# A gated convolution block with an MLP on one core: a short convolution in 8 steps of 16 channels, a skip term added before the transposes, two more tiles through the transposing DMA, paired 64-row matmuls, and a new order

## The chip, the core and the metric

One core of a Trainium2 chip runs the whole program. The metric is the time of one execution on the device in microseconds (us), the median of several runs. The engines have these names: PE (TensorE, matmuls; PEld are its weight loads), DVE (VectorE), ACT (ScalarE), POOL (GpSimd) and SP, which here issues DMAs. Each engine works through its own list of instructions in order; semaphores make one wait for another. PE writes to PSUM, which has 8 banks here (128 partitions x 512 float32 columns); only DVE and ACT empty them.

## The reference

S = 2048 positions, D = 640 channels, F = 1728, all inputs bfloat16:

```python
x = A_q
# A: short convolution, gate, long convolution, skip term, gate
k_shift[t] = sum(k[t - j] * shift_k[:, j] for j in range(4))      # per channel
kv = k_shift * v
y  = long_conv(kv, ssm_k) + kv * ssm_D                            # causal, 2048 taps, per channel (an FFT in the reference)
h  = x + layernorm(x) * y
# B: MLP
a  = layernorm(h) @ w1 + b1;  act = a * tanh(softplus(a))         # Mish
out = h + act @ w2
```

## The kernel before

The long convolution is done as matmuls with constant tables, in two steps forward (128 x 16), a product per frequency, and two steps back. `s1kpe`, `s1vpe` are the first forward step of the filter and of `kv` (lines L543 and L544: pairs of matmuls that each use 64 columns of the array and run together), `s2kpe` (L652) and `s2vpe` (L685) the second with the 4 MB table `g`, `p1_`/`p2_` (L706, L710) the products, `i1pe` (L743, L744) and `i2pa/b/c` (L803) the way back. `k1pe` (L625) transposes the filter, `ktpe` (L571) transposes k. Channels go in five blocks of 128 that form chunks 0 (blocks 0, 1), 1 (2, 3) and 2 (4). `sw` are DMAs inside SBUF that swap neighbouring partitions of the filter's spectrum for the complex product.

The short convolution `kspe` (L595, L596) multiplies transposed k with banded matrices `wsh`, which POOL builds (L501) from `coef`, a spread-out copy of shift_k (L493). Four steps of 32 channels by 4 times: a first matmul of 128 columns and a second of 96 columns that brings in the time steps before. `kv` (L600, DVE) takes the result out of PSUM and multiplies it by v. The skip term is one addition to the transposed filter's first row, `dadd` (L620), behind the `k1` transposes.

After the way back, for each of 16 tiles of 128 positions: `y` moves it out of PSUM (L419 on ACT, L421 on DVE), `wb` (L813) multiplies by the normed x (`lnx`, L790 on ACT or L792 on POOL), `h` (L817) adds x, `bn` (L822 to L824) and `pow` (L827, POOL) give the statistics, `hc` (L832) the normed tile. Tiles 0 to 3 are transposed by PE (`trpe`, L850) and copied (`trev`), tiles 4 to 15 by a transposing DMA (`trd`, L839). The MLP runs in five units of 256, 256, 512, 512, 512 positions: `m1pe` (L898) is the first matmul for 13 blocks of 128 hidden values, `m1pex` (L878) that for the last 64 of 1728 (two halves of positions together), `hb`/`hbx` (L903, L881) Mish on ACT, `m2pe` (L915, L916) the second matmul with 14 accumulating steps for each half of a tile, `res` (L921) the residual and `d_out` the way out. The 14th step (L916) holds 64 hidden values and 64 rows of zeros, which POOL writes (`w2z`, `w2hz`).

What runs where and in which order is written out by hand: the string `ORDER` names some 700 operations with an engine letter (t PE, a ACT, v DVE, p POOL, d a DMA issued by SP, s one issued by ACT). `_schedule` gives each a start from a table of costs and sorts by it; the lists of the engines come out of that. SP's DMAs are one list too: a DMA whose wait is not over holds up all behind it. `fz` and `wm` are matmuls on zeros whose results nothing uses. A POOL product that overlaps DVE's products is put behind them by a copy into `turn` (L936), since `_schedule` gives products of the two engines one port.

Of the kernel before, what the change touches and what calls it, by code (L numbers as in the profile page):

```python
# [17 lines left out]
D = 640  # L18
# [8 lines left out]
d_id:s d_sk:s wz:v d_dr:s cz:v d_go:d d_n2:d wm:t fz0:t d_n0:d k1pe2x:t warm:a k1ev2x:a d_n3:d k1pe2y:t d_n1:d cfpe:t d_n4:d k1pe0y:t k1ev0y:a  # L27
k1pe0x:t k1ev2y:v dadd2:v s1kpe2_0x:t k1ev0x:v kz:p coef:v s1kpe2_2x:t s1kpe2_1x:t s1kpe2_1y:t s1kev2_1x:v s1kev2_0x:v s1kev2_1y:v s1kpe2_3y:t
s1kev2_3y:a k1pe3x:t k1ev3x:a s1kev2_2x:a k1pe1x:t k1ev1x:v k1pe1y:t w2hz:p dadd0:p wsh0:p dadd1:p k1pe3y:t dadd3:p k1pe4y:t k1ev1y:v k1pe4x:t
k1ev3y:v k1ev4x:v dadd4:p s1kpe1_2y:t k1ev4y:a s1kpe1_3x:t s1kpe1_0x:t s1kev1_0x:v s1kpe1_0y:t s1kpe1_1x:t s1kev1_1x:v s1kpe0_1x:t s1kpe1_3y:t  # L30
s1kpe4_0y:t s1kev1_2y:a s1kpe2_2y:t s1kev1_3x:a d_k3:d d_k2:d d_x0:d s1kev0_1x:a s1kev1_0y:v s1kev1_3y:a s1kev2_2y:a s1kpe3_0x:t s1kpe0_2y:t
s1kev0_2y:a s1kpe0_1y:t s1kev3_0x:a s1kpe2_3x:t s1kev2_3x:a ktpe3y:t s1kpe0_2x:t s1kpe4_2x:t s1kev4_2x:a s1kev4_0y:v ln1_2:v s1kev0_1y:v ln1_1:v
s1kpe4_1x:t s1kpe0_0x:t s1kev4_1x:a s1kpe4_2y:t s1kpe1_2x:t s1kev0_0x:v s1kpe0_0y:t d_k1:d d_g4:d s1kev1_2x:a d_k0:d d_g5:d s1kpe3_2x:t ktpe0y:t
s1kev0_2x:a ktpe1y:t d_v1:d ktev0y:v ktpe4y:t ktev3y:v s1kpe4_0x:t ktev1y:v ktev4y:v s1kev4_2y:a s1kev0_0y:a s1kev3_2x:a s1kpe3_1y:t s1kev4_0x:a
s1kev3_1y:a s1kpe3_3x:t s1kpe3_0y:t s1kpe4_1y:t s1kev3_3x:a s1kpe0_3y:t s1kpe4_3y:t s1kpe2_0y:t s1kpe4_3x:t s1kev0_3y:v s1kev2_0y:v s1kev4_1y:a
ln1_3:v s1kev3_0y:a s1kev4_3x:a wsh1:p s1kpe3_2y:t ln1p1:p s1kpe3_1x:t s1kpe1_1y:t ktsh1:p wsh3:p s1kpe0_3x:t s1kpe3_3y:t s1kev3_1x:a ktpe2y:t
s1kev0_3x:a s1kev4_3y:a s1kev3_2y:v s1kev1_1y:v ktpe4x:t ktpe3x:t ktev3x:v ktpe1x:t s1kev3_3y:a ktev1x:v ln1_0:v ktpe0x:t s2kpe_14y:t d_g6:d d_g0:d
ktev2y:a ktpe2x:t d_g7:d d_g1:d ktev4x:a s2kpe_13x:t s2kev_13x:a s2kpe_15y:t s2kpe_12y:t s2kev_12y:a ktev0x:a s2kev_15y:a kspe4_1x:t ktev2x:v kv4_1x:v
kspe1_1y:t s2kpe_11y:t kv1_1y:v kspe1_1x:t s2kev_11y:a kspe4_1y:t kv1_1x:v s2kpe_1y:t s2kev_1y:a kv4_1y:v ktsh0:p wsh2:p s2kpe_12x:t kspe0_1y:t
kv0_1y:v s2kpe_13y:t s2kpe_16y:t kspe3_1x:t s2kpe_16x:t kv3_1x:v s2kev_12x:a s2kev_14y:a s2kev_16x:v d_v0:d s2kev_16y:a d_g3:d s2kev_13y:a kspe0_1x:t  # L40
kv0_1x:v s2kpe_19y:t d_g2:d ktsh4:p s2kpe_0y:t s2kpe_0x:t s2kev_0x:a s2kpe_1x:t s2kev_1x:a s2kev_0y:a d_small:p ktsh3:p s2kev_19y:a ktsh2:p kspe3_1y:t
kv3_1y:v kspe2_1x:t s2kpe_18x:t s2kev_18x:a s2kpe_20y:t kv2_1x:v s2kpe_17x:t s2kpe_18y:t s2kpe_17y:t s2kpe_4y:t s2kev_17x:a s2kev_20y:v s2kpe_3x:t
# [132 lines left out]
def _schedule(ops):  # L175
# [7 lines left out]
    for word in ORDER:  # L183
# [32 lines left out]
        for rt in o.allocs:  # L216
            rt.ring.take(rt.slot, rt)
# [751 lines left out]
```

## Time and profile before

| | us |
|---|---|
| median of 3 runs (224.56 to 224.84) | 224.58 |
| the profiled execution | 224.86 |
| its span, first to last instruction | 223.1 |
| PE busy | 214.7 (96%) |
| DVE busy | 146.2 (66%) |
| ACT busy | 134.4 (60%) |
| POOL busy | 65.7 (29%) |

The granted TensorE clock is 1.000 throughout. "Busy" of PE counts the overlapping lengths of pipelined matmuls (a 128-column one is 219 ns long, but the next starts 56 ns later), so a PE that is always busy can still issue less than it could. Starts in the timeline show the rate. The span starts with the first instruction; some 1.8 us of the execution lie outside it.

### The profile page before, as it was taken

What the parts mean: (1) busy time and instruction counts of PE and PEld (TensorE: products, weight loads), DVE (VectorE), ACT (ScalarE), POOL (GpSimd) and SP (SyncE); (2) the same over time, 40 slices, a digit from 0 to 9 for tenths busy, and PEclk for the clock granted to TensorE, in tenths of its full rate; (3) what the DMA queues carried; (4) which work ended last, traced back from release to release, by engine and by line L of the source; (5) the groups of instructions that cost most, each with busy time, mean ns of one, the idle gap of its engine ahead of it and who ended that gap; (6) DMA issues with size and microseconds to landing.
All of it is one profiled execution on the core that took longest, in us unless ns stands there. A gap on an engine that the chain in (4) does not pass through costs nothing.

```text
span 223.1 us, 6218 instructions
## 1 busy us (share of the span) xinstructions
PE 214.7 (96%) x2598; PEld 162.1 (73%) x2598; DVE 146.2 (66%) x317; ACT 134.4 (60%) x268; POOL 65.7 (29%) x106
## 2 busy tenths in 40 slices
PE   7998899999999999999999999999999999999994
PEld 2988899999877999988887644576645445675773
DVE  0699989999999998999788898974400000004023
ACT  2689989999999999888870446800053454330000
POOL 1271950005596007235767714320000000000000
PEclk9999999999999999999999999999999999999999
DMA  6999991075999999100001401043350000000024
GB/s 214 388 408 424 408 413 69 3 203 193 277 290 283 319 351 347 62 3 0 3 0 32 88 0 31 0 91 60 88 179 0 1 0 3 0 0 0 32 82 153
DMA packets 27342, 30.68 MB, mean 138 GB/s; under 512 B 9393, under 2 KB 23730, under 8 KB 26930
## 3 DMA queue, kind: packets, MB, share of 16 engines
q1 hardware_dynamic: 26880, 30.10, 41.1%
q8 instruction: 20, 0.33, 0.6%
q10 hardware_dynamic: 338, 0.18, 0.3%
q14 instruction: 8, 0.07, 0.1%
q0 software_dynamic: 96, 0.00, 0.0%
HBM read 20.45 MB, written 2.62 MB: 103 GB/s over the span
## 4 chain that ended last, share of the span: by engine, by line
PE 64%; DVE 13%; DMA 7%; ACT 7%; POOL 5%; issue 2%; SPq 0%; DVEq 0%; ACTq 0%; POOLq 0%
PE ps L915 21%; PE ps L898 19%; ACT uv L419 6%; DMA x<-in_A_q_dram 5%; PE ps L743 4%; PE ps L744 4%; PE ps L652 3%; PE ps L543 2%; PE ps L571 2%; DMA rn<-in_A_ssm_k_dram 2%; DVE st L776 2%; DVE st L822 2%; PE ps L595 2%; POOL r L782 2%; PE ps L916 2%
## 5 line engine op out<-in xcount | busy, mean ns | idle before, releaser
L915 PE MATMUL ps<-rn,uv 128*128 128x320 bf16 (+2 forms) x416 | 61.1, 299 | 0.2 <-DVE x L921 0.2
L903 ACT ACTIVATE uv<-ps,b1s 128x512 bf16<-128x512 f32 (+1 forms) x65 | 35.4, 610 | 39.1 <-PE ps L898 38.5
L898 PE MATMUL ps<-G 128*128 128x512 bf16 (+1 forms) x325 | 58.6, 337 | 0.0
L915 PEld LDWEIGHTS <-uv 128*128 128x128 bf16 x416 | 40.2, 98 | 17.5 <-issue 0.4
L419 ACT CAST uk<-ps 128x512 bf16<-128x512 f32 (+1 forms) x96 | 48.7, 702 | 2.6 <-PE ps L544 1.6
L898 PEld LDWEIGHTS <-G 128*128 128x128 bf16 x325 | 31.2, 98 | 23.9 <-issue 1.1
L921 DVE TENSOR_TENSOR xb<-ps,xb 128x320 bf16<-128x320 f32 (+2 forms) x12 | 5.7, 487 | 36.3 <-PE ps L916 35.8
L419 ACT CAST uv<-ps 128x512 bf16<-128x512 f32 (+2 forms) x57 | 28.7, 845 | 0.0
L921 DVE TENSOR_TENSOR xa<-ps,xa 128x320 bf16<-128x320 f32 x12 | 5.9, 488 | 21.6 <-PE ps L916 21.6
L827 POOL TENSOR_TENSOR r<-ve,mhalf 128x1 f32<-128x1 f32 x16 | 10.0, 630 | 32.7 <-DVE ve L824 32.7
L743 PE MATMUL ps<-a,uv 128*128 128x128 bf16 x160 | 18.8, 219 | 0.2
L421 DVE CAST uk<-ps 128x512 bf16<-128x512 f32 (+1 forms) x27 | 17.2, 669 | 1.4 <-PE ps L744 0.9
L743 PEld LDWEIGHTS <-uv 128*128 128x128 bf16 x160 | 17.9, 113 | 0.0
L421 DVE CAST uv<-ps 128x512 bf16<-128x512 f32 (+1 forms) x25 | 15.3, 677 | 0.0
L685 PE MATMUL ps<-uv,G 128*128 128x64 bf16 (+1 forms) x256 | 12.8, 197 | 0.8
L685 PEld LDWEIGHTS <-G 128*128 128x128 bf16 x256 | 11.1, 96 | 3.1 <-issue 2.1
L600 DVE TENSOR_TENSOR ra<-ps,rb 128x512 bf16<-128x512 f32 x20 | 12.5, 684 | 0.3 <-PE ps L596 0.3
L419 ACT CAST rb<-ps 128x512 bf16<-128x512 f32 (+1 forms) x28 | 10.6, 495 | 2.7 <-PE ps L803 2.7
L652 PE MATMUL ps<-uk,G 128*128 128x160 bf16 x128 | 12.1, 230 | 0.0
L782 POOL TENSOR_TENSOR r<-ve,mhalf 128x1 f32<-128x1 f32 x16 | 10.8, 672 | 1.3
L706 DVE TENSOR_TENSOR uv<-uv,uk 128x2048 bf16<-128x2048 bf16 (+1 forms) x11 | 10.9, 1022 | 0.0
L544 PE MATMUL ps<-cst,ra 128*64 128x128 bf16 x160 | 10.6, 220 | 0.1
(116 smaller groups left out, 376.7 us busy)
## 6 DMA issues: line engine op xcount, KB each, us to landing
G<-tab_g SPq DMA_DIRECT2D x8, 512.0 KB, 12.9
rn<-in_A_ssm_k_dram SPq DMA_DIRECT2D x5, 512.0 KB, 6.2
ra<-in_A_k_dram SPq DMA_DIRECT2D x4, 640.0 KB, 9.9
rb<-in_A_v_dram SPq DMA_DIRECT2D x2, 1280.0 KB, 13.1
G<-in_B_w_dram SPq DMA_DIRECT2D x5, 432.0 KB, 6.4
rn<-in_B_w_dram SPq DMA_DIRECT2D x1, 2080.0 KB, 9.8
rn<-uk SPq DMA_DIRECT2D x4, 512.0 KB, 5.1
rb<-uk SPq DMA_DIRECT2D x8, 256.0 KB, 7.9
```

The costliest lines, as they stand in the source:

```text
L419: nc.scalar.copy(o, i)
L421: nc.vector.tensor_copy(o, i)
L600: nc.vector.tensor_tensor(kv_w[:, m, :, 8 * h:8 * h + 8, l0:l0 + n], ps.rearrange("p (l t d) -> p d t l", l=n, t=8), raw_v[:, 8 * h:8 * h ...
L652: nc.tensor.matmul(ps[:, o:o + 160], g_v[:, f, :], KA[:, :, f, :], start=True, stop=True)
L685: nc.tensor.matmul(ps[:, fl * n:fl * n + n], g_v[:, f0 + h * kf + fl, :], VX[x][:, :, f0 + h * kf + fl, :], start=True, stop=True)
L706: eng.tensor_tensor(v, v, K[c.i][:, :, f0:f1, :], ALU.mult)
L743: nc.tensor.matmul(pz[:, k, :], V[c.i][:, dg // 4, :, dg % 4], a12[:, 0, :], start=True, stop=False)
L782: nc.gpsimd.tensor_tensor(r1[:, t2:t2 + 1], ve1[:, t2:t2 + 1], mhalf[:, 0:1], ALU.pow)
L898: nc.tensor.matmul(ph[:, 0:w], w1[:, dc, fc * P:fc * P + P], lnhT_of(u)[:, dc, 0:w], start=(dc == 0), stop=(dc == NDC - 1))
L903: nc.scalar.activation(hb_of(u)[:, fc, 0:w], rt.tile[:, 0:w], ACT.Mish, bias=b1s[:, fc:fc + 1], scale=1.0)
L915: nc.tensor.matmul(po[:, 0:d1 - d0], hb_of(u)[:, fc, tl * P:(tl + 1) * P], w2[:, fc, d0:d1], start=(fc == 0), stop=False)
L921: nc.vector.tensor_tensor(x, rt.tile[:, 0:d1 - d0], x, ALU.add)
```

## The change

- **Short convolution.** 8 steps of 16 channels. k is transposed so that a bank holds channels of one parity; the second matmul has 48 columns instead of 96. `wsh` is 10 pieces of 704 columns (5 blocks, 2 parities) instead of 4 of 1120; five of them lie in the `uv` tiles, five in `xb`. `coef` comes out of nine small matmuls (`cfpe`) as one copy of 440 columns; before, it was a memset and four copies. `ktsh`, the shift by one row on POOL, has 1016 elements instead of 508.
- **Skip term.** Four small matmuls (`dcpe`) and a copy (`dcev`, 5 columns) spread ssm_D over the partitions, and `dq` (DVE, 128 x 1, five times) adds it to the filter before the transposes; the `dadd` go.
- **Tiles 2 and 3** are transposed by DMA (`trd2`, `trd3`).
- **The last 64 hidden values.** `m2q` multiplies them first, for two tiles at a time: each matmul uses 64 rows of the array, one tile the lower half, the other the upper, with 4 banks taken per pair. `m2pe` keeps 13 steps. The zero rows and their memsets go. `m1pex` does each unit by itself in the same number of columns.
- **Products of chunk 0** in 8 pieces of 1024 elements instead of 4 of 2048, and their `sw` DMAs in 4 pieces instead of 2.
- **Loads.** Half of the first filter block comes from ACT's queue. `fz` is two matmuls instead of one, `wm` 8 instead of 9.
- **Order.** All of `ORDER` is new. On SP the filter blocks come first, then x0 after one quarter of k, v earlier, the table g in the order of use; `w2` is behind `trd3`, where before it stood ahead of x1. Of the products POOL has 9 of 1024 elements (before 2 of 2048), and DVE 23 of 1024 and 4 of 2048 (before 16 and 10).

```diff
-ORDER = """d_id:s d_sk:s wz:v d_dr:s cz:v d_go:d d_n2:d wm:t fz0:t d_n0:d k1pe2x:t ...
+ORDER = """wz:v kz:p d_id:s d_sk:s d_go:d d_n0:d d_n1:d wm:t dcpe:t dcev:v dq0:v fz1:t k1pe0y:t k1pe0x:t cfpe:t ...
...
+    for a in range(4):   # emit_dc
+        nc.tensor.matmul(ps_f32(dc_rt)[:, 0:NDC], cst[0:32, 4 * P + 3 - a:5 * P + 3 - a], d_row[:, a:20:4], start=(a == 0), stop=(a == 3))
...
-            m = mk.unsqueeze(1).to_broadcast([P, 35, 32])
+            out = wsh[m][k].rearrange("p l (t d) -> p (l t) d", d=16)
+            a = mk.unsqueeze(1).to_broadcast([P, 44, 16])
...
-                        nc.tensor.matmul(o, t[:, l, a, :], wsh[r // 5][:, r % 5, 0:128], start=True, stop=False)
-                        nc.tensor.matmul(o[:, 0:96], t[:, l, a - 1 if a else 4, :], wsh[r // 5][:, r % 5, 128:224], start=False, stop=True)
+                    nc.tensor.matmul(o, t[:, q, h, :], w[:, 0:128], start=True, stop=False)
+                    nc.tensor.matmul(o[:, 0:48], t[:, q, 0 if h else 2, :], w[:, 128:176], start=False, stop=True)
...
-            k = kd[0:1, 0]
-            (nc.vector if e == "dve" else nc.gpsimd).tensor_tensor(k, k, rd, ALU.add)
+            nc.vector.tensor_tensor(n[:, 0:1], n[:, 0:1], d_col[:, b:b + 1], ALU.add)
...
-        npf = (32, 32, 32)[len(c.dcs) - 1]
+        npf = (16, 32, 32)[c.i]
...
-        if U_OF[t2] >= 2:
+        if U_OF[t2] >= 1:
...
+            def pq(e, ab=ab, parts=parts):
+                for i in range(2):
+                    for t2 in ab:
+                        _, c, h = last64[t2]
+                        d0, d1, rt = parts[t2][i]
+                        rhs = w2h[64:P, d0:d1] if h else w2[0:64, 13, d0:d1]
+                        nc.tensor.matmul(ps_f32(rt)[:, 0:d1 - d0], hbx[64 * h:64 * h + 64, c:c + P], rhs, start=True, stop=False)
...
-                    for fc in range(NFC - 1):
-                        nc.tensor.matmul(po[:, 0:d1 - d0], hb_of(u)[:, fc, tl * P:(tl + 1) * P], w2[:, fc, d0:d1], start=(fc == 0), stop=False)
-                    nc.tensor.matmul(po[:, 0:d1 - d0], lhs, w2h[:, d0:d1] if h else w2[:, 13, d0:d1], start=False, stop=True)
+                    for fc in range(NFC - 1):
+                        nc.tensor.matmul(po[:, 0:d1 - d0], hb_of(u)[:, fc, tl * P:(tl + 1) * P], w2[:, fc, d0:d1], start=False, stop=(fc == NFC - 2))
```

More of the change, by code (lines that the diff above doesn't have):

```diff
@@ L26 @@
 ORDER = """
[L27 to L30, printed above, removed]
@@ L71 @@
-i2pa2:t i1ev2_3x:v y0a:a ln1_15:v i2pc0:t y0b:v i2pc1:t y1a:a ln1p2:p lnx0:p lnx2:p i2pa9:t y1b:a wb0:v wb1:v i2pa12:t h0:v h1:v bn0:v bn1:v i2pb2:t
-i2pa6:t i2pa8:t i2pb6:t i2pa3:t i2pa11:t pow0:p y6a:a i2pa15:t i2pb11:t i2pb15:t i2pb3:t hc0:v i2pc2:t pow1:p y2a:a d_x1:d y11a:a y15a:v i2pa14:t
-i2pb8:t y2b:a y3a:a hc1:v i2pb14:t i2pb12:t i2pa10:t i2pa7:t i2pc3:t y14a:a y12a:a y8a:a y3b:a i2pb9:t i2pb10:t i2pa5:t i2pc6:t y6b:a i2pb7:t i2pb5:t
-i2pc7:t trpe0:t i2pa13:t i2pa4:t y9a:a trev0:v trpe1:t y7a:a y10a:a y7b:v trev1:v wb3:v wb2:v h3:v i2pc11:t i2pb4:t i2pc12:t i2pc9:t i2pb13:t
@@ L75 @@
-m1pe0_9:t y5a:a y4a:a y11b:a hb0_9:a h2:v bn2:v bn3:v ln1p15:p m1pe0_4:t y9b:a m1pe0_5:t m1pe0_3:t m1pe0_6:t i2pc4:t y4b:a hb0_6:a m1pe0_11:t
-m1pe0_2:t pow2:p hc2:v m1pe0_0:t pow3:p ln1_6:v hc3:v y12b:a m1pe0_10:t ln1p6:p lnx6:p ln1_12:v ln1_4:v ln1_5:v hb0_5:a y13a:a hb0_4:a hb0_10:a w2z:p
-trpe2:t hb0_0:a hb0_2:a trev2:a m1pe0_7:t ln1p5:p m1pe0_8:t trpe3:t trev3:a ln1p4:p m1pe0_12:t m1pe0_1:t hb0_7:a hb0_8:a hb0_1:a hb0_3:a m1pex0:t
-m1pe1_8:t wb6:v h6:v m1pe1_11:t ln1_8:v hb0_12:a i2pc8:t lnx4:p m1pe1_10:t y8b:a hb0_11:a hb1_11:a m1pe1_7:t hb1_7:a m1pe1_2:t m1pe1_5:t m1pe1_6:t
@@ L95 @@
-d_out12:d d_out8:d d_out4:d d_out13:d
+wz:v kz:p d_id:s d_sk:s d_go:d d_n0:d d_n1:d wm:t dcpe:t dcev:v dq0:v fz1:t k1pe0y:t k1pe0x:t cfpe:t k1pe1y:t warm:a k1ev0x:v k1ev0y:a s1kpe0_3y:t
+s1kev0_3y:a s1kpe0_2y:t s1kpe0_0x:t coef:v wsh4_0:p wsh1_1:p wsh2_0:p dq1:v wsh0_0:p wsh3_0:p wsh1_0:p s1kpe0_0y:t d_n3:d d_n2:d s1kpe0_1y:t
+s1kpe0_3x:t s1kpe0_1x:t k1ev1y:a wsh2_1:p wsh4_1:p wsh3_1:p wsh0_1:p s1kev0_0y:v dq3:v s1kev0_0x:v dq2:v d_n4:d d_k3:d d_x0:d d_k2:d k1pe1x:t k1pe2y:t
+k1pe2x:t s1kev0_1y:a k1ev1x:a k1ev2y:v dq4:v k1pe3y:t k1pe3x:t k1ev3y:v k1ev2x:v k1ev3x:a fz0:t s1kev0_3x:a s1kpe1_2y:t s1kpe1_1y:t s1kev0_1x:v d_k0:d
@@ new lines @@
+i1ev1_2y:v i1ev2_3x:v i1pe2_2y:t i1ev2_2y:v i2pa0:t i2pa1:t i2pb0:t i2pa2:t i2pb1:t y1a:a i2pc0:t i2pc1:t y1b:a i2pa7:t y0a:v y0b:v wb0:v wb1:v
+i2pb2:t i2pa8:t y2a:a c_b1:a h0:v h1:v bn0:v bn1:v d_w10:d d_w13:d i2pb7:t d_w12:d d_x1:d d_w11:d y7a:a pow0:p i2pa3:t i2pb8:t i2pa9:t i2pc2:t i2pb3:t
+y3a:a i2pa4:t i2pb9:t i2pc6:t i2pa12:t y2b:a i2pb4:t y8a:a pow1:p i2pa10:t hc0:v i2pa6:t i2pa11:t i2pa13:t i2pb6:t y9a:a y4a:a y6a:a i2pb11:t i2pa5:t
+i2pb10:t i2pb13:t i2pc3:t y6b:a y3b:a wb2:v y13a:a hc1:v fz2:t trpe0:t i2pa15:t i2pa14:t wb3:v h2:v trpe1:t h3:v bn2:v trev0:a pow2:p bn3:v pow3:p
@@ new lines @@
+i2pb14:t i2pb15:t i2pb5:t i2pb12:t trev1:a i2pc4:t y4b:a m1pe0_7:t y14a:a m1pe0_6:t hb0_7:a hc2:v trd2:d hc3:v trd3:d ln1_6:v y15a:a d_w2:d hb0_6:a
+y10a:a ln1p11:p ln1p6:p m1pe0_0:t m1pe0_2:t m1pe0_11:t i2pc5:t y11a:a y5a:a hb0_2:a hb0_0:a m1pe0_4:t m1pe0_3:t i2pc14:t m1pe0_1:t hb0_4:a y5b:v
+hb0_3:a ln1_7:v hb0_11:a lnx6:p ln1p7:p ln1_4:v ln1_5:v lnx11:p ln1p5:p y14b:v m1pe0_5:t m1pe0_12:t hb0_12:a i2pc13:t y13b:v m1pe0_10:t y12a:a hb0_5:a
+ln1_12:v ln1_8:v i2pc11:t m1pe0_9:t m1pe0_8:t i2pc8:t hb0_10:a m1pe1_11:t y11b:a hb1_11:a hb0_1:a lnx5:p m1pe1_4:t y8b:v m1pe1_3:t hb0_8:a hb1_3:a
@@ L187, in _schedule @@
         dur = dict(o.opts)[eng]
-        est = max([free.get(eng, 0.0)] + [d.finish + d.lat + _TAIL[d.eng] + _HOP for d in o.deps])
+        est = max([free.get(eng, 0.0)] + [d.finish + (0.0 if d.eng == eng and eng.startswith("dma") else d.lat + _TAIL[d.eng] + _HOP) for d in o.deps])
         base = est
@@ L191, in _schedule @@
             t, rt.slot = rt.ring.free()
+            rt.ring.take(rt.slot, rt)
             est = max(est, t)
@@ L204, in _schedule @@
                     t = fetched
-                fetched = t + (_SLOW if free.get("dma", 0.0) > t + 0.3 else _FETCH)
+                fetched = t + next(d for end, d in _FETCH if t < end)
                 mark += _BLOCK
@@ L327 @@
     turn = cpool.tile([P, 1], BF16, name="turn")
-    sk_r = cpool.tile([32, 80], BF16, name="sk_r")
-    coef = cpool.tile([P, 20, 7], BF16, name="coef")
+    sk_r = cpool.tile([16, 160], BF16, name="sk_r")
+    d_col = cpool.tile([P, NDC], BF16, name="d_col")
+    d_row = cpool.tile([32, 20], BF16, name="d_row")
+    coef = cpool.tile([P, 440], BF16, name="coef")
     st1 = cpool.tile([P, NT, 2, 6], F32, name="st1")
@@ L530 @@
     d_go = OP("d_go", ("dma", 0.75))
-    d_n = [DMA(f"d_n{b}", P * S * 2, emit_kn(b), deps=[d_go], lat=3.1) for b in range(NDC)]
+    d_n = [DMA("d_n0", P * S * 2, emit_kn(0), deps=[d_go], rate=405e3, lat=3.0)]
+    d_n += [DMA(f"d_n{b}", P * S * 2, emit_kn(b), deps=d_n[:1], rate=405e3, lat=3.45) for b in range(1, NDC)]
+    for o in d_k + d_v:
+        o.deps.append(d_n[0])
     s1_pes = [[] for _ in CHUNKS]
@@ L584, in shf @@
         def shf(e, t=kt_s[b]):
-            nc.gpsimd.tensor_copy(t[:, :, 4, 1:128], t[:, :, 3, 0:127])
-        kts.append((o_ev, OP(f"ktsh{b}", ("pool", 0.61), [o for o in o_ev if not o.name.endswith("x")], emit=shf, prio=9)))
+            nc.gpsimd.tensor_copy(t[:, :, 2, 1:128], t[:, :, 1, 0:127])
+        kts.append((o_ev, OP(f"ktsh{b}", ("pool", 1.1), [o for o in o_ev if not o.name.endswith("x")], emit=shf, prio=9)))
     for m in range(NDC):
@@ L605 @@
             ks_pe_all += o_pe
             kv_ops[m] += o_kv
-    d_g = [DMA(f"d_g{i}", 0.525e6, emit_g(i), prio=0.6, lat=4.9) for i in range(8)]
+    d_g = [DMA(f"d_g{i}", 0.525e6, emit_g(i), deps=d_n[:1], prio=0.6, lat=4.9) for i in range(8)]
     d_small = OP("d_small", ("pool", 3.0), kts[0][0], emit=emit_small2, lat=6.0)
@@ L712 @@
             extra = 0.06 * (len(SW[c.i]) - 1)
[L713 removed]
+            p2 = OP(f"p2_{c.i}_{i}", [("dve", _dve2(npf * n) + extra), ("pool", _pool2(npf * n) + extra)], need + [o for k, o in enumerate(sw_ops[c.i]) if k * P // len(sw_ops[c.i]) < f1 and (k + 1) * P // len(sw_ops[c.i]) > f0], emit=(lambda e, fn=fn: fn(e, which=1)), prio=15 + c.i)
             p2.probe = SW[c.i][-1][1][:, 0, f1 - 1, 0:1]
@@ L754, in emit_x @@
         return lambda: nc.sync.dma_start((x0, xa, xb)[h][:, 0:(4, 6, 6)[h] * D].rearrange("p (a d) -> p a d", d=D), xview[:, (0, 4, 10)[h]:(4, 10, 16)[h], :])
-    d_x = [DMA(f"d_x{h}", (0.66e6, 0.98e6, 0.98e6)[h], emit_x(h), deps=((), i1_pes[1], ks_pe_all)[h], prio=3.5 if h else 0.55, lat=2.5 if h else 3.4) for h in range(3)]
+    d_x = [DMA(f"d_x{h}", (0.66e6, 0.98e6, 0.98e6)[h], emit_x(h), deps=(d_n[:1], i1_pes[1], ks_pe_all)[h], prio=3.5 if h else 0.55, lat=2.5 if h else 3.4) for h in range(3)]
     def emit_w2():
```

284 lines of the change are left out of this document (146 added, 138 removed).

## Prediction

> **What bounds the kernel now.** First the page's 40 slices, then busy time by stretch.
>
> ```profile
> PE   7998899999999999999999999999999999999994
> DVE  0699989999999998999788898974400000004023
> ACT  2689989999999999888870446800053454330000
> DMA  6999991075999999100001401043350000000024
> ```
>
> PE looks full everywhere, so the other rows divide the span: DVE and ACT are full too until about slice 15, and fall off after.
>
> ```profile
> core 0: us, PE busy (x) PEld busy (x) DVE busy (x) ACT busy (x) POOL busy (x), PEclk, DMA share, GB/s
> 5.70:28.00 22.30, 20.39 (x472) 19.32 (x473) 19.72 (x41) 19.05 (x33) 12.58 (x14) 1.00 1.02 407
> 28.00:50.00 22.00, 22.00 (x452) 21.43 (x451) 21.23 (x37) 21.19 (x46) 3.17 (x7) 1.00 0.49 173
> 50.00:72.70 22.70, 21.11 (x464) 18.36 (x462) 22.54 (x32) 22.70 (x50) 14.94 (x9) 1.00 0.90 259
> 72.70:124.00 51.30, 51.16 (x612) 45.37 (x612) 46.53 (x115) 39.98 (x92) 23.50 (x46) 1.00 0.37 121
> 124.00:220.00 96.00, 95.87 (x595) 56.30 (x594) 35.36 (x94) 30.00 (x49) 10.48 (x21) 1.00 0.16 41
> ```
>
> Up to 72.7 us the copies out of PSUM bind: DVE and ACT stand still for 7.4 us of engine time between 5.7 and 50 us and for 0.2 us between 50 and 72.7. From 72.7 us PE binds; DVE and ACT have room. The chain of waits gives PE's rate there, start to start, and the cost of going over to matmuls on half the array:
>
> ```profile
> 51.02 0.96 PE ps L685 x32
> ...
> 128.10 3.36 PE ps L898 x15
> 131.46 0.67 PE ps L878 x10
> ...
> 143.13 1.77 PE ps L915 x13
> 145.03 1.77 PE ps L915 x13
> ...
> 168.88 14.03 PE ps L898 x65
> ```
>
> A 512-column matmul costs 14.03/65 = 0.216 us, a 320-column one 1.77/13 = 0.136, a 64-column one 0.03. The 15 before L878 take 3.36 where 15 x 0.216 = 3.24: 0.12 is the way in. The 10 halves of 256 columns run in pairs, 5 x 0.109 = 0.55, and take 0.67: 0.12 is the way out. So a visit costs 0.24.
>
> **The change, part by part.** Two sums, since only what the bound engine saves counts.
>
> *PE's stretch, after 72.7 us.* (1) The 14th step goes: 30 x 0.136 + 0.216 + 0.056 = 4.35. The pairs cost half that, 2.18, if they overlap as the column halves of L878 do, and eight visits cost 8 x 0.24 = 1.92: net -0.25. No row shows row halves; the bounds are 2.18 less (switches free) and 2.18 more (no overlap); I take L878's row as the nearest. (2) `trpe2`, `trpe3`: 10 transposes at 0.056 us, start to start: -0.56. What hides the DMA instead (2.6 us from issue to landing, SP 1.2 us each) is `m1pe0`. With hc1's end as zero, DVE needs 0.8 for two `h` and 0.4 for a `wb`, 2.6 for two `bn` and 0.4 for `hc2`: 4.2. `hc3` ends at 4.8, its DMA is issued by 5.5 and lands at 8.1. PE reaches unit 1 after `trpe1` and `trev1` (1.5), 13 x 0.545 and five `i2pc` (0.11 each): 9.1. Cover 1.0 us, so nothing is charged. (3) `fz2` doubles ahead of `trpe0`: +0.2 of its 0.43, as PE waits there for `hc0` in part. (4) `w2` is now issued behind `trd3`, at 6.7. It is 2.2 MB; x1 moved at 404 GB/s (7,680-byte packets), w2's 1,280-byte packets at about 370, so 6 us and some 2 us to start and end: 14.7 to 15. PE comes to `m2q0`, which needs its last rows, after eight `m1pe1` and `m1pex0`: 9.1 + 8 x 0.545 + 0.79 + 0.11 = 14.4. All of `m1pe1` and `m2pe` queues behind it: +0.5. Sum: -0.25 - 0.56 + 0.2 + 0.5 = **-0.1**.
>
> *The copies' stretch, before.* (5) DVE's products: from 10 x 1.14 + 16 x 0.60 = 21.0 to 4 x 1.14 + 23 x 0.60 = 18.4: -2.6; POOL takes nine halves of the 4.1 us that L710 shows, 18.4 instead of 8.1, in a stretch where it is busy 15 of 45 us. (6) `coef`: four copies of 0.24 and a 0.175 memset become one copy of about 0.55: -0.6; the DVE `dadd`, -0.2. (7) `dq` and `dcev`: six small DVE instructions at 0.15 (a 128x1 row): +0.9. Together -2.5 for two engines that share the copies: **-1.2**. (8) The 48 columns save PE 80 x (0.042 - 0.029) = 1.0, where PE is not the bound: 0 (bound -1.0). `cfpe`, `dcpe`, `wm` lie ahead of the first landing: 0. `wsh` is 10 x 1.3 = 13 us of POOL instead of 8.3, `ktsh` 1.2 instead of 0.61; the first user, `kspe0_1y`, comes behind all filter blocks, near 28 us: 0. (9) `dq0` stands ahead of `k1pe0x`: a copy, an addition, two hops: +0.2; `k1pe0y` covers the rest. (10) `dq1` to `dq4` have two operands in SBUF and run while POOL builds `wsh`. The timelines of POOL and DVE show what that does:
>
> ```profile
> 114.02 0.87 POOL L792 TENSOR_SCALAR ra<-xa,r,nmr 128x640 bf16<-128x640 bf16 x1
> 114.29 0.94 DVE L813 TENSOR_TENSOR rb<-rb,ra 128x640 bf16<-128x640 bf16 x1
> 116.03 0.48 DVE L813 TENSOR_TENSOR rb<-rb,ra 128x640 bf16<-128x640 bf16 x1
> ```
>
> The addition that met POOL's instruction took 0.94 instead of 0.48. Each `dq` can wait out a piece of `wsh`: 0 to 1.3, mean 0.65, and the copies behind it on DVE wait too, with PE behind those banks. 4 x 0.65 = 2.6 on DVE, some of it in idle time that is there anyway: +0.6. The Trainium skill (SBUF — State Buffer, section "Who interferes with whom") says that a DVE instruction with two SBUF inputs and a GpSimd one that reads SBUF exclude each other for the whole instruction; by that rule all four wait and the term is nearer its upper end. (11) The order. Of the 7.4 idle us some 2.1 are the wait for the first bank (ACT 6.48, DVE 6.98); 5.3 are left, with the wait for x0 (0.6 on DVE) and a stall of PE's instruction supply (0.8 at L571) among them. x0 now comes one k quarter earlier, v before most of g, and the chunk 0 path starts ahead of the filter's last blocks. I let half be filled, 5.3 / 2 / 2 = -1.3; ends 0 and -2.65, or +2 if the new lists stall elsewhere. (12) Quarters of `sw0` have 256-byte pieces: the transposes' 256-byte packets took 18 ns, the swaps' 512-byte ones 28, so 2 MB cost 9.2 us of DMA instead of 7.2, beside a DMA that the 28 to 50 stretch shows half idle: 0. Sum: -1.2 + 0.2 + 0.6 - 1.3 = **-1.7**.
>
> The profiled execution, 224.86, becomes 224.86 - 1.8 = 223.06; it stood 0.28 over the median: 222.8.
>
> **Rivals.**
>
> *Slower, w2 late.* In before w2's last pieces landed 8.3 and 9.7 us after issue, on a busy DMA. If they do so here, from 7.9, they land at 16.2 to 17.6 and PE stands at `m2q0` until then: 3.2 us instead of 0.5, so 225.5. It decides from a wait of 2.3 on, which eats the whole gain. Against it: DMA is idle then (0.03 of its time from 90 to 100 us). Chance 0.14.
>
> *Slower, the shared port.* By the skill's rule above, as this kernel's mechanism: four `dq` wait 1.3 each (5.2), and DVE's products beside POOL's three late ones another 2. DVE, in order, is then 7 late against 2.5 saved, and ACT cannot take its copies: +4.5 instead of -0.6 for terms 5 to 7 and 10, halved where ACT has spare banks: 225.6. For it: the 0.94 above. Against: at 63 to 70 us POOL's small instructions, not DVE's, were stretched. 0.14.
>
> *The pairs do not pair.* Row halves in one column pass run one after the other: +2.18, 225.0, within 0.2% of now. 0.10.
>
> *More gain.* Idle time all filled, no lock, free switches: -1.35 - 0.6 - 1.9 - 0.5 = 218.4. The new lists may also take PE's stalls of 50 to 72.7 us (22.7 less 21.11 busy, more by start times). 0.18.
>
> **Numbers.** Forecast 222.8, chance 0.44. About 0.2%, 0.45 us, is what a measurement of this kernel can tell from no change. Faster: 0.44 + 0.18 = 0.62; same 0.10; slower 0.28. The range takes in both slow rivals with the bound of term 11 and most of the gain: 218.4 to 226.4; the forecast's own case spans 220.5 to 224.1.
>
> **What would show it.** Right: 13 steps in 1.77 us with 16 pairs at 0.136 and 0.24 per visit; DVE and ACT idle under 6 us from 5.7 to 50; PE full from about 71 us; under 1 us of wait for a DMA at `m2q0`. Wrong: `dq` rows of 0.6 us and more, PE waiting for `w2` or for a transposed tile, 0.27 us between pairs, or DVE waiting in 50 to 73 us.

## The result, and the profile after

| | before | after |
|---|---|---|
| median, us | 224.57 (224.19 to 224.84, 4 runs) | 232.76 (231.92 to 234.07, 4 runs) |
| profiled execution, its span | 224.86, 223.1 | 234.07, 232.3 |
| granted TensorE clock | 1.000 | 0.978 |

The ratio is 1.0371, 95% interval 1.0320 to 1.0422: slower by 8.2 us. The forecast was 222.8.

The 40 slices of the page, changed kernel (tenths; one slice is 5.8 us):

```profile
PE   7689999999988999999959999999999999999994
...
DVE  0269999999999999998976678935341000032131
ACT  2156998999999999899862232830113287300000
...
PEclk9679999999999999999988999999999999999999
DMA  6999179434499990512921610243024000000034
```

Two places stand out (slices counted from 0), and PEclk, which was 9 throughout before, marks both: slices 1 and 2, where DVE and ACT are half idle, and slice 20, where PE falls to 5 and the clock to 8 for two slices. The windows put sizes to them (columns as in the prediction; the last three are granted clock, DMA share, GB/s):

```profile
5.70:28.00 22.30, 19.03 (x323) 17.05 (x324) 14.90 (x29) 12.91 (x20) 13.31 (x10) 0.85 0.84 329
28.00:50.00 22.00, 21.60 (x502) 20.18 (x497) 21.40 (x38) 21.27 (x45) 10.08 (x16) 1.00 0.69 233
...
72.70:124.00 51.30, 48.29 (x629) 43.19 (x629) 48.21 (x113) 44.83 (x99) 22.25 (x39) 0.97 0.55 182
```

From 5.7 to 28 us DVE has 14.9 us of work done (before 19.72), ACT 12.9 (before 19.05), at a clock of 0.85. After that the stages run at their old pace: the first `kspe` starts at 35.27 instead of 29.42, 5.9 later; the first `m1pe` at 103.76 instead of 98.05, 5.7 later. From there to the end it takes 128.5 instead of 125.05, and what is lost lies around the first `m2q`.

PE's waits name both (engine, line and what it waited for: us in total, times, longest):

```profile
PE ps L930 <- ACT uv L914: 2.8, 1, 2.8
PE ps L634 <- DMA rn<-in_A_ssm_k_dram: 2.4, 1, 2.4
...
PE ps L634 <- DVE rn L628: 1.0, 1, 1.0
```

L634 is `k1pe`, waiting for the first filter block and then for `dq` (L628); L930 is `m2q`. The DMA issues show why the first block is late: of its two halves the one in ACT's queue, third there, is issued at 1.63 and takes 6.2 us, to 7.9; SP's half, issued at 0.72, lands at 4.6.

```profile
rn<-in_A_ssm_k_dram SPq DMA_DIRECT2D x1, 256.0 KB, 3.9
rn<-in_A_ssm_k_dram ACTq DMA_DIRECT2D x1, 256.0 KB, 6.2
```

The first `s1kpe` pairs start 0.107 us apart (12.2 to 14.9 us) and 0.056 in the groups after 19 us; before they were at 0.056 in the first group already. The chain shows the same thing behind the second wait, and further on a visit to `m2q` in its normal state:

```profile
120.26 1.74 PE ps L909 x10
122.00 2.89 PE ps L942 x13
...
125.55 1.77 PE ps L942 x13
127.32 1.09 PE ps L909 x10
...
130.18 0.38 PE ps L930 x4
130.55 1.87 PE ps L942 x13
```

Ten `m1pe` matmuls take 1.74 instead of 1.09, a half tile of `m2pe` 2.89 instead of 1.77: 1.8 us lost after the wait was over.

### The profile page after: what moved, and what is told of

The parts are those of the page before. It is cut to its first block, busy times and chain, and to the rows that moved or that the text cites. A ratio compares the mean times of both kernels' runs of the same rounds, so it can differ in the third digit from the quotient of the medians.

```text
span 232.3 us, 6302 instructions
## 1 busy us (share of the span) xinstructions
PE 219.9 (95%) x2623; PEld 162.3 (70%) x2623; DVE 146.7 (63%) x324; ACT 133.2 (57%) x261; POOL 78.9 (34%) x114
## 4 chain that ended last, share of the span: by engine, by line
PE 55%; POOL 5%; DVE 4%; issue 1%; ACT 1%; DVEq 0%; POOLq 0%
PE ps L942 25%; PE ps L909 20%; PE ps L754 4%; PE ps L755 4%; POOL r L791 2%; PE ps L930 1%; DVE st L831 1%; POOL ra L801 1%; POOL nmr L792 1%; PE ps L889 1%; POOL ve L790 1%; DVE x L826 1%; POOL r L836 1%; DVE rb L822 0%; ACT ra L799 0%
## 5 line engine op out<-in xcount | busy, mean ns | idle before, releaser
L942 PE MATMUL ps<-rn,uv 128*128 128x320 bf16 (+2 forms) x416 | 59.9, 303 | 0.0
L909 PE MATMUL ps<-G 128*128 128x512 bf16 (+1 forms) x325 | 59.7, 339 | 0.0
L914 ACT ACTIVATE uv<-ps,b1s 128x512 bf16<-128x512 f32 (+1 forms) x65 | 35.5, 611 | 41.9 <-PE ps L909 41.8
L422 ACT CAST uk<-ps 128x512 bf16<-128x512 f32 (+2 forms) x92 | 49.2, 760 | 3.8 <-PE ps L562 3.1
L422 ACT CAST uv<-ps 128x512 bf16<-128x512 f32 (+2 forms) x57 | 30.8, 812 | 0.0
L836 POOL TENSOR_TENSOR r<-ve,mhalf 128x1 f32<-128x1 f32 x16 | 9.3, 588 | 38.7 <-DVE ve L833 38.7
L424 DVE CAST uk<-ps 128x512 bf16<-128x512 f32 (+1 forms) x31 | 20.0, 668 | 2.8 <-PE ps L562 2.4
L721 POOL TENSOR_TENSOR rn<-rn,uv 128x1024 bf16<-128x1024 bf16 x5 | 10.6, 2128 | 11.5 <-PE ps L609 11.1
L696 PE MATMUL ps<-uv,G 128*128 128x64 bf16 (+1 forms) x256 | 12.9, 197 | 1.2 <-ACT uv L422 0.6
L422 ACT CAST rb<-ps 128x512 bf16<-128x512 f32 (+1 forms) x24 | 10.0, 483 | 6.6 <-PE ps L812 6.6
L661 PE MATMUL ps<-uk,G 128*128 128x160 bf16 x128 | 13.1, 230 | 0.4 <-DVE uk L424 0.4
L561 PE MATMUL ps<-cst,ra 128*64 128x128 bf16 x160 | 11.0, 219 | 0.2
L562 PE MATMUL ps<-cst,ra 128*64 128x128 bf16 x160 | 11.1, 222 | 0.0
## 6 DMA issues: line engine op xcount, KB each, us to landing
rn<-in_B_w_dram SPq DMA_DIRECT2D x1, 2080.0 KB, 10.2
```

Of the source, the lines that this page charges most:

```text
L422: nc.scalar.copy(o, i)
L424: nc.vector.tensor_copy(o, i)
L562: nc.tensor.matmul(ps[64:128, k, :], lhs, ms, start=True, stop=True)
L661: nc.tensor.matmul(ps[:, o:o + 160], g_v[:, f, :], KA[:, :, f, :], start=True, stop=True)
L696: nc.tensor.matmul(ps[:, fl * n:fl * n + n], g_v[:, f0 + h * kf + fl, :], VX[x][:, :, f0 + h * kf + fl, :], start=True, stop=True)
L836: emit=(lambda e, t2=t2: nc.gpsimd.tensor_tensor(r2[:, t2:t2 + 1], ve2[:, t2:t2 + 1], mhalf[:, 0:1], ALU.pow)), prio=pr - 0.1)
```

## The experiments

The theory at the outset: a late landing at the start and a late `w2`, each followed by a spell at half the clock. Its rivals: POOL's `wsh` holding up DVE's `dq`, and the new order itself. For `m2q` the page named a fourth bank that ACT frees (`hb`, L914, ends 119.6) and the DMA rows named `w2` (119.4 to 119.8). Letters in the expectations are those of the single run.

**First filter block whole**

```diff
-        nc.scalar.dma_start(raw_n[0][64:P], n_view[0, 16:32])
-        return lambda: nc.sync.dma_start(raw_n[b], n_view[b]) if b else nc.sync.dma_start(raw_n[0][0:64], n_view[0, 0:16])
+        return lambda: nc.sync.dma_start(raw_n[b], n_view[b])
```

> One edit on the changed kernel: filter block 0 comes whole by SP's queue (one 512 KB transfer), not its second half by ACT's queue behind two other transfers. Theory A (the late second half, and the low granted clock that follows PE's wait for it, cost the start): the first matmul on the filter moves from 7.96 to 5.7 to 6.3, PE's wait of 2.4 ahead of it goes, the matmuls after it run at the full granted clock, and the first kspe comes at 30 to 33 instead of 35.3; time 227 to 230 against 232.8. Rival B (the start only moves waiting; DVE's additions beside POOL's wsh, or the pieces of the new order, set the pace of the first 35 us): the first matmul moves by 2, kspe by under 1, time 232 to 233.

229.64 (227.41 to 230.20, 4 runs; ratio to before 1.0199, 1.0134 to 1.0264). First filter matmul at 5.80, granted clock 1.00 from 5.7 to 28, `s1kpe` at 0.056 in its first group, first `kspe` at 30.77: 4.5 earlier. That is theory A of this run; what its rival may still claim is the 1.3 us to the first `kspe` of before (29.42).

**Zero matmuls in the wait.** In the first try the count hung on a loop variable that had its last value when the matmuls were emitted, so it stayed at two, and the run measures the changed kernel again: 233.28 (231.62 to 234.28).

> One edit on the changed kernel: the group of zero matmuls ahead of the first filter matmul is 14 long instead of 2, so PE is busy while it waits for filter block 0; the landing stays where it is, at 7.9. If the granted clock of the first 15 us is low because PE had stood idle, the half speed pairs (0.106 us start to start for s1k from 12.2 to 14.9) become 0.055 and the first kspe comes 1.5 to 3 earlier: 229.5 to 231.3. If the clock falls for another reason (power of all engines together, the chip's temperature), nothing moves: 232 to 233. If only the landing counts: nothing moves either, but the pairs at 0.055 would still be seen.

The second try:

```diff
-emit=lambda e, rt=fz_rt: [nc.tensor.matmul(...) for _ in range(2)])
+emit=lambda e, rt=fz_rt, n={1: 14}.get(i, 2): [nc.tensor.matmul(...) for _ in range(n)])
```

> One edit on the changed kernel, and the one that the run fill_start was meant to be (there the number of zero matmuls had not changed, so it is a repeat of the changed kernel): 14 zero matmuls of 512 columns instead of 2 ahead of the first filter matmul, about 3 us of PE at full rate, in the wait for filter block 0. The landing stays at 7.9. If the low clock of the next 7 us comes from PE having stood idle, the s1k pairs run at 0.055 us start to start instead of 0.106 from 12 us on, and the first kspe comes 1.5 to 3 earlier: 229.8 to 231.5. If the landing and the work behind it set the pace, the pairs run at 0.055 but kspe moves by under 0.7: 232.3 to 233.

231.72 (230.33 to 232.91). The first filter matmul starts at 8.13, as late as before the edit, yet the pairs run at 0.056 from 10.8 us on, and the first `kspe` comes at 32.83 instead of 35.27. So of the 4.5 us that the whole block gives, 2.4 are the clock and 2.1 the landing. Only 1.0 reached the end: the wait at `m2q` and a longer slow spell behind it took the rest (below).

**`w2` first, and `lnx4` later**

```diff
-d_w10:d d_w13:d i2pb7:t d_w12:d d_x1:d d_w11:d ... hc3:v trd3:d ln1_6:v y15a:a d_w2:d
+d_w10:d d_w13:d i2pb7:t d_w12:d d_w11:d d_w2:d d_x1:d ... hc3:v trd3:d ln1_6:v y15a:a
```

> One edit on the changed kernel: SP issues w2 ahead of x1 and of the two transposing DMAs, in the place it had before the change. Theory A (at the first m2q pair the wait of 2.9 has two causes that end within 0.5 us of each other: w2's last rows, 119.4 to 119.8, and the fourth bank, freed by ACT's hb at 119.1): w2 lands 5 or more earlier, and the wait shrinks by 0.3 to 0.7 only; time 232 to 232.8. Rival B (w2 alone holds the pair): the wait goes to 0.5, the low granted clock behind it goes too, time 228 to 229. Third: x1 and the transposed tiles now land later, and the wait shows up at m1pe1 or the first residual: 233 or more.

```diff
-ln1p4:p lnx4:a m1pe1_8:t hb1_8:a m2q0:t
+ln1p4:p m1pe1_8:t hb1_8:a lnx4:a m2q0:t
```

> One edit on the changed kernel: on ACT, lnx4 stands behind hb1_8 instead of ahead of it, so hb does not stand behind ACT's wait for POOL's nmr. Theory A (two causes end together): hb ends near 118 instead of 119.1, the fourth bank is free 1 us sooner, but w2's last rows still land at 119.4 to 119.8: time 232 to 233. Rival B (the banks alone hold the pair): PE's wait falls from 2.9 to about 1.7: 230.5 to 231.7.

With `w2` first: 229.77 (229.03 to 231.06), 3.0 less; no wait at `m2q`, clock 1.00 from 116 to 126. With `lnx4` later: 233.48 (232.69 to 234.25), no gain. The theory of two causes that end together fell: `w2` alone held `m2q`. The timeline of `w2_first` says why the page's releaser was wrong:

```profile
116.53 0.31 PE L930 MATMUL ps<-rn,hbx 64*128 64x320 bf16 x1
...
118.89 0.45 ACT L914 ACTIVATE uv<-ps,b1s 128x256 bf16<-128x256 f32 x1
```

The `hb` that was named as releaser ends 2.8 us *after* `m2q` has started. In the changed kernel it merely ended in the same half microsecond as the DMA. The same wait in `fill_start_2` is put down to the DMA:

```profile
PE ps L930 <- DMA rn<-in_B_w_dram: 2.9, 1, 2.9
```

**`dq` with one tensor input**

```diff
-    d_col = cpool.tile([P, NDC], BF16, name="d_col")
-            nc.vector.tensor_tensor(n[:, 0:1], n[:, 0:1], d_col[:, b:b + 1], ALU.add)
+    d_col = cpool.tile([P, NDC], F32, name="d_col")
+            nc.vector.tensor_scalar(n[:, 0:1], n[:, 0:1], d_col[:, b:b + 1], None, ALU.add)
```

> One edit on the changed kernel: dq is an instruction with one tensor input and a per-partition scalar operand, not two tensor inputs; the sum is the same. Theory A (lock: a DVE instruction with two tensor inputs in SBUF waits out POOL's piece of wsh): the three rows of 1.27, 0.80 and 0.81 us become 0.2 or less, DVE gets 2.3 us back in the first 20 us, of which half comes through to the first kspe; time 231 to 232.3 against 232.8. Rival B (the rows are long for another reason, such as the instruction's own start or the wait for the filter block): they stay above 0.6 and nothing moves. Rival C: the rows get short, but PE and ACT wait for filter blocks anyway: 232.8.

232.45 (230.91 to 233.89). The rows shrink as theory A says. First the third `dq` in DVE's timeline of the changed kernel and the pieces of `wsh` in POOL's, then the same `dq` in this run:

```profile
14.77 1.27 DVE L628 TENSOR_TENSOR rn<-rn,d_col 128x1 bf16<-128x1 bf16 x1
...
14.65 5.35 POOL L516 TENSOR_TENSOR uv<-cst,coef 128x704 bf16<-128x704 bf16 x4
```

```profile
14.85 0.21 DVE L628 TENSOR_SCALAR rn<-rn,d_col 128x1 bf16<-128x1 bf16 x1
```

In the changed kernel each of the three long rows ends within 0.02 us of a piece of `wsh`: 16.04, 17.36 and 18.69 against 16.02, 17.34 and 18.67. The first two, at 7.95 and 11.83, are over before POOL's first piece starts at 12.00, and take 0.15 to 0.16. With one tensor input all five take 0.21 to 0.22, also while a piece is running. The first `kspe` comes 1.2 earlier, but a change of the median by 0.3 can't be told from none among these runs; the next two show it better.

**Both repairs, and all three**

> Both edits that moved the time: filter block 0 whole by SP's queue, and w2 issued ahead of x1 and of the transposing DMAs. Alone they gave -3.1 (229.64) and -3.0 (229.77) from 232.8. Theory (two separate losses, 110 us apart): they add, 226.2 to 227. Rival (after an earlier start something else stands at the first m2q pair, such as the fourth bank that ACT frees 2.4 us after that pair began in the run w2_first, or x1): 227.5 to 229.

> Both edits, and dq with a scalar operand. In the run e1_whole_block three dq rows take 1.14, 0.80 and 0.81 at 10.4 to 13.4, PE then waits 1.35 for one, and ACT 2.55 for PE. Theory (the lock is the third loss): rows of 0.2, first kspe about 1 to 1.5 earlier than 30.77, time 1 to 1.5 below the run e1_w2, so 224.9 to 226: level with the kernel before or at most 0.6% above. Rival (the pieces of the new order and DMA landings set the first 30 us): within 0.4 of e1_w2.

The whole block and `w2` first: 225.62 (10 runs; ratio 1.0037, 1.0012 to 1.0063): 7.1 less than the changed kernel, where the two alone add up to 6.1; the difference is within the spread of the changed kernel's runs (2.1). With `dq` too: 224.06 (223.67 to 224.84, 12 runs; ratio 0.997, 0.9947 to 0.9993), 1.6 less again. The first `kspe` moves from 30.97 to 29.23; PE's wait of 1.35 for `dq` and ACT's of 2.6 for PE become none and 1.03. Three edits take back all of the 8.2 us and 0.5 more. The copies' stretch of this kernel:

```profile
5.70:28.00 22.30, 22.15 (x454) 19.94 (x453) 18.61 (x40) 18.87 (x32) 18.66 (x20) 1.00 0.96 377
28.00:50.00 22.00, 21.61 (x497) 20.61 (x497) 21.66 (x37) 21.27 (x47) 10.58 (x10) 1.00 0.66 204
```

DVE and ACT are idle for 44.3 - 40.27 + 44.3 - 40.14 = 8.2 us of engine time from 5.7 to 50, before 7.4.

**The half first in ACT's queue**

```diff
+        nc.scalar.dma_start(raw_n[0][64:P], n_view[0, 16:32])
         nc.scalar.dma_start(cst[:], dram["cst"])
         nc.scalar.dma_start(d_row[:], A_ssm_D.rearrange("(d r) -> d r", r=20))
-        nc.scalar.dma_start(raw_n[0][64:P], n_view[0, 16:32])
-wm:t dcpe:t dcev:v dq0:v fz1:t k1pe0y:t k1pe0x:t
+wm:t fz1:t k1pe0y:t dcpe:t dcev:v dq0:v k1pe0x:t
```

> The kernel of e1_w2_dq, but filter block 0 stays in two halves, as the change has it: the half of ACT's queue is now the first transfer there, not the third, and on PE the four matmuls on d_row (dcpe) stand behind k1pe0y instead of ahead of it. Theory (the late landing came from the half's place behind two transfers and behind four 512 KB blocks of SP's queue, not from ACT's queue as such): the half lands by 5 instead of 7.9, the first filter matmul comes at 4.9 to 5.7 instead of 6.1, no low clock; time 223.2 to 224.2. Rival (a transfer of ACT's queue is late wherever it stands there): first matmul at 6.5 or later, 225 or more.

227.15 (226.97 to 227.78, 6 runs). The theory missed, and of the rival only the time came true: the first filter matmul starts at 6.00. The half does land by 4.6, so ACT's queue is not slow as such, but what now stands behind it is late:

```profile
rn<-in_A_ssm_k_dram ACTq DMA_DIRECT2D x1, 256.0 KB, 3.9
cst<-tab_cst ACTq DMA_DIRECT2D x1, 161.0 KB, 4.5
d_row<-in_A_ssm_D_dram ACTq DMA_DIRECT2D x1, 1.2 KB, 5.2
```

`cst`, which the transposes need, lands at 5.9 (2.9 in the changed kernel), `d_row` at 7.3; `k1pe0x` waits for the `dq` behind it until 8.07, and the clock from 5.7 to 28 is 0.92. What counts is the last landing of several that the first matmuls need.

**The split alone, in the kernel before**

```diff
         nc.scalar.dma_start(sk_r[:], A_shift_k.rearrange("(d n) j -> d (n j)", n=20))
+        nc.scalar.dma_start(raw_n[2][64:P], A_ssm_k.rearrange("(d m l) s -> m d l s", m=NDC, l=4)[2, 16:32])
...
+        return lambda: nc.sync.dma_start(raw_n[b], v[b]) if b != 2 else nc.sync.dma_start(raw_n[2][0:64], v[2, 0:16])
```

First with block 0, then with block 2 (shown):

> The kernel before the change, with one part of the change alone: filter block 0 in two halves, the second as the third transfer of ACT's queue. Theory (late half plus the low clock after PE's wait, 4.5 us of the start in the changed kernel, 3.1 to 4.5 of its time): first filter matmul from 5.7 to about 7.9, granted clock under 0.9 from 5.7 to 28, time 227 to 229 against 224.7. Rival 1 (the landing alone): +2.0 to 2.4, clock 1.0, 226.7 to 227.1. Rival 2 (the loss needs the new order): under +1.

> The kernel before the change, with its first filter block in two halves, the second as the third transfer of ACT's queue. In the run before_split it was block 0 that was split, and the order of before begins with block 2, so PE had other work until 7.1 and lost 0.35 there; here it is block 2. Theory (a wait for the first block costs its length and the low clock that follows): first filter matmul at 7.3 to 7.9 instead of 5.7, low granted clock behind it, 227 to 229 against 224.6. Rival 1 (landing alone, PE keeps its clock): +1.6 to 2.2. Rival 2 (the old order hides it behind DVE's and ACT's later idle time): under +1.

Block 0: 225.83 (ratio 1.0051, 1.0035 to 1.0068), clock 1.00, some 1.2 slower: the theory missed, because the old order begins with block 2, and PE starts on block 0 only 0.35 late (7.36 instead of 7.01). Block 2: 228.11 (227.31 to 228.73; ratio 1.0138, 1.0102 to 1.0175), 3.4 slower:

```profile
7.65 1.18 PE L627 MATMUL ps<-cst,rn 128*128 128x128 bf16 x16 [1.96 <-DMA rn<-in_A_ssm_k_dram]
```

```profile
5.70:28.00 22.30, 20.34 (x453) 19.32 (x454) 17.69 (x37) 16.56 (x30) 10.50 (x13) 0.92 1.02 404
```

So the loss of the start needs nothing of the new order but this: that the split block is the one PE begins with.

**Two terms of PE's sum**, each undone in the kernel of `e1_w2_dq`:

```diff
-                for i in range(2):
-                    for t2 in ab:
+                for t2 in ab:
+                    for i in range(2):
```

> The kernel of e1_w2_dq, with the four matmuls of each m2q in the order first row half twice, second row half twice, so that at most one of the three neighbours in a visit uses the other half of the rows. Theory (row halves overlap when they are neighbours): a visit goes from 0.378 to about 0.51 us, 8 x 0.136 = 1.1 in all: 224.7 to 225.3. Rival (the short visits come from something else, the order doesn't matter): 224.06 plus or minus 0.3.

```diff
-hc2:v trd2:d hc3:v trd3:d ... m1pe0_12:t hb0_12:a ... m1pe0_9:t
+hc2:v hc3:v ... m1pe0_12:t trpe2:t trev2:a hb0_12:a ... trpe3:t trev3:a m1pe0_9:t
...
-        if U_OF[t2] >= 1:
+        if t2 >= 4:
```

> The kernel of e1_w2_dq, with tiles 2 and 3 transposed on PE again (10 matmuls and two copies on ACT) instead of by the transposing DMA. The prediction's step: 10 x 0.056 = 0.56 more on PE, nothing else: 224.4 to 224.9. Rival (ACT's two copies or the wait for hc3 hold m1pe1 up): 225 to 226. Other rival (PE waited in this stretch anyway): no change, 224.06 within 0.3.

The pairs: 224.07, no change, a miss. A visit takes 0.381 instead of 0.378 us. The timeline shows the matmuls out of the order in which they stand (written: `rn`, `rn`, `w2h`, `w2h`; `rn` is the lower half of the rows, `w2h` the upper):

```profile
120.10 0.31 PE L929 MATMUL ps<-rn,hbx 64*128 64x320 bf16 x1
120.11 0.31 PE L929 MATMUL ps<-w2h,hbx 64*128 64x320 bf16 x1
120.25 0.30 PE L929 MATMUL ps<-rn,hbx 64*128 64x320 bf16 x1
120.26 0.30 PE L929 MATMUL ps<-w2h,hbx 64*128 64x320 bf16 x1
```

The transposes: 224.86 over 12 runs (224.10 to 228.31), 224.74 without the two at 228.3; ratio 1.0004, 0.9989 to 1.0019. That is about 0.7 slower than `e1_w2_dq`, where 0.56 was worked out. The profiled execution is one of the two at 228.3: its `s1kpe` pairs start 0.107 us apart until 13.6, so it is left aside for the transposes.

**Zero matmuls ahead of `dcpe`**, in the kernel of `e1_w2_dq`:

```diff
-wm:t dcpe:t dcev:v dq0:v fz1:t k1pe0y:t
+wm:t fz1:t dcpe:t dcev:v dq0:v k1pe0y:t
```

> The kernel of e1_w2_dq, with the two zero matmuls (fz1) ahead of the four matmuls on d_row (dcpe) instead of behind them. In e1_w2_dq PE waits 0.39 for d_row at 4.8 to 5.2, then runs fz1 from 5.41 to 6.08, and only then the first filter matmul, whose block had landed by 5.7. Theory (fz1 now fills the wait for d_row, so PE is not idle while its clock is coming up, and the first filter matmul comes at 5.6 to 5.8): 0.3 to 0.5 off, 223.5 to 223.8, and fewer executions with a slow start. Rival (the first k1 copies wait for dq0 and the banks, not for PE): 224.06 within 0.2.

223.97 (223.81 to 224.33, 12 runs; ratio 0.9964, 0.9948 to 0.9980). First filter matmul at 5.74, `kspe` 0.2 earlier, but the median within 0.1 of `e1_w2_dq`, as the rival has it. With this and the three repairs the change gains 0.4% on the kernel before.

## Why the prediction was wrong

The forecast is missed by 10.0 us: 3.1 are the first block's place in the queues and 3.0 that of `w2`, each with the low clock behind the wait, 1.0 more goes when both are undone together (within the spread of the runs), 1.6 are the lock, and 1.3 are a gain that did not come (224.06 with the three repairs, 222.8 forecast).

**The start was not costed.** The change says that half of the first filter block comes from ACT's queue. The sum has no term for it; the text only sets `cfpe`, `dcpe` and `wm` "ahead of the first landing: 0", as if that landing stayed where it was. Cost: 4.5 us to the first `kspe`, 3.1 of the median. The trace of before had a row to ask with: the second transfer of ACT's queue, 5 KB of shift_k, took 3.8 us to land beside the 512 KB blocks of SP's queue.

**The granted clock was not in the sum.** It was 1.00 in every row of before, and a wait was priced at its length. Here a wait of PE cost its length and up to as much again: 2.4 after the start, 1.8 at `m2q`. The Trainium skill (TensorE: Matmul & The Clock Gate, Part 1, "What's actually happening") says that PE runs at half clock by default, keeps the full one only while it is busy, and that the decision falls in free-running windows of about 3.4 us. The 0.107 and 0.056 us between pairs agree with it, and so do the lengths of the low spells: at half speed, a mean clock of 0.83 from 116 to 126 us stands for 3.4 us, 0.66 there in `fill_start_2` for 6.8, and 0.85 from 5.7 to 28 for 6.7, one or two such windows each. That waits of 2.4 to 2.9 us, shorter than such a window, sufficed here does not follow from it.

**Step 4, `w2`, was mis-sized.** Issue 6.8 us after hc1's end was as forecast (109.21 against 102.43), and PE at `m2q` at 14.4 (116.85) as well. The landing was 17.0 to 17.4, not 14.7 to 15: the pieces took 9.0 to 10.2 us, not 6 and some 2. From 112 to 117 us DMA moved 341 to 383 GB/s, as forecast, so what was too small is the start and the end. The rival "w2 late" had that mechanism and 16.2 to 17.6; the argument against it, an idle DMA, was true (share 0.00 to 0.10 from 102 to 108 us) but did not help, and its price left out the clock. Wait 2.8 instead of 0.5, and 1.8 behind it.

**Step 10, the lock, was right in kind and too small.** The last three `dq` lasted 2.4 over their 0.15 together (forecast 2.6 for four), and no longer than 0.22 with one tensor input. But "some of it in idle time that is there anyway" left too little: 1.6 came through where +0.6 was taken, as PE waited for `dq` and ACT for PE. This is the rule of the Trainium skill that the prediction weighed (SBUF — State Buffer, "Who interferes with whom"), and the traces bear it out. They also agree with the same section's other half, that an instruction with at most one SBUF input, outside the two-port modes, keeps clear of it; the per-partition scalar did not count as a second input here. The rest of the rival "shared port" was hardly put to the test: only one of DVE's products overlaps one of POOL's in the changed kernel, by 0.2 us, and it took 0.77; the others of 1024 elements took 0.68 to 0.69, as before.

**Step 11, the order, brought nothing.** Idle time was 8.2 us after the repairs against 7.4; half of 5.3 was to go. Step 5 was right in size (products 20.7 us instead of 23.2, -2.5 for -2.6), but from 5.7 us to the first `i2pa` (88.87 before, 89.16 with the repairs) DVE and ACT together were busy for 157.3 and 157.7 us: other instructions took the room, among them two more `BATCH_NORM_STATS2` on DVE (12, before 10), three more copies there (67, before 64; ACT has two fewer) and a `lnx` on ACT. The end of `s2vpe` did come 1.1 earlier, the first `i2pa` not. Here the prediction's line is also less sharp than it took it: it let PE alone bind from 72.7 on, by a row that runs to 124, but up to 89 ACT is as full as PE, as the finer window of before shows:

```profile
72.70:89.00 16.30, 16.25 (x282) 16.07 (x282) 14.81 (x24) 16.14 (x34) 3.83 (x8) 1.00 1.02 338
```

ACT works 16.14 of 16.30 there, and PE's 282 matmuls at 0.056 us from start to start fill 15.8. With the repairs DVE and ACT work 16.02 and 16.26 of the same stretch. Which of the two keeps the first `i2pa` where it is, and which of these instructions could have been left for later, wasn't tried; that part of the missing gain stays open.

**What was right.** Step 1: a visit to `m2q` costs 0.10 on the way in (0.232 between starts instead of 0.136), two pairs of 0.136 and 0.11 on the way out, so 0.20 over its pairs where 0.24 was taken: 8 visits and the pairs cost 3.8 against 4.35, -0.6 for -0.25. "The pairs do not pair" is refuted by the visit of 0.38, which would be 0.54 and more. Step 2: no wait for tiles 2 and 3, and 0.7 for 0.56. Step 9: the first copies 0.3 later (forecast 0.2). PE's stretch from the first `m1pe` to the end lasts 124.8 us with the repairs, 125.05 before: -0.3, where steps 1 to 3 were to make -0.6 and with the sizes measured for steps 1 and 2 would make about -1.0. Where the rest of it went is not shown.

## What to carry to other kernels

A change that regroups loads is costed from the first instruction on: for each of the first matmuls, which transfer lands last, and where that transfer now stands in its queue. A wait of PE is priced with the low clock that can follow it. And a releaser that ends within half a microsecond of a DMA is a guess until one of the two is moved: here it was the DMA.

## What the runs showed that was not expected

- **The price of a wait is not a function of its length alone.** At `m2q` a wait of 2.50 (`dq_scalar`) cost nothing more: the ten `m1pe` behind it took 1.10 from start to start. Waits of 2.44 (`fill_start`), 2.56 (`e1_whole_block`) and 2.78 (the changed kernel) cost 1.7 each by the starts behind them (1.8 by the chain), one of 2.87 (`fill_start_2`) 2.6. In `act_half_first` the clock fell after three waits of 0.3 to 0.6 close together. What decides is not shown. Whether this makes the spread of the changed kernel, 231.9 to 234.1, beside 223.8 to 224.3 of `zero_first`, stays open: its four runs list mean clocks of 0.978, 0.985, 0.985 and 1.000 and took 234.07, 232.82, 231.92 and 232.71.
- **The granted clock of a row can miss a low spell.** In `transposes_on_pe` the row from 5.7 to 28 us reads 1.00, although the `s1kpe` pairs start 0.107 us apart from 10.7 to 13.6. The distance between starts is the safer sign.
- **Matmuls on different halves of the rows pass each other**, as the rows of `pairs_serial` show: the second line in time is not the second in the program, whose first two are both `rn`. The Trainium skill (TensorE: Matmul & The Clock Gate, Part 3, "The mechanism") has matmuls start and end in program order; here they did not.
- **A place further forward in one queue is paid for behind it**: 256 KB ahead of `cst` made a 161 KB transfer land 3.0 us later.
